# Loading, inverting and using the first batch's sums one double step sooner in a routed attention kernel with a feed-forward block

## The chip, the cores and the metric

The kernel runs on one core of one Trainium2 chip. Its time is device time in microseconds (us) from launch to end, as the median of several runs.

## The reference

Attention with routing, then a feed-forward block on its output, all in float32:

```python
batch, n_heads, seq, head_dim = (4, 8, 768, 64); n_clusters = 16
q_assign = np.argmax(np.einsum('bhsd,hcd->bhsc', q_n, c_n), axis=-1)   # same for k_assign
mask = q_assign[:, :, :, None] == k_assign[:, :, None, :]
scores = scale * np.matmul(q, k.transpose(0, 1, 3, 2))
scores = np.where(mask, scores, -1000000000.0)
scores = scores - np.max(scores, axis=-1, keepdims=True)
attn = np.exp(scores)
attn = attn / (np.sum(attn, axis=-1, keepdims=True) + 1e-09)
attn_out = np.matmul(attn, v)
x = attn_out.transpose(0, 2, 1, 3).reshape(3072, 512)
h = x @ w_in                        # 512 -> 2048
g = h * np.clip(h + 3.0, 0.0, 6.0) / 6.0
out = g @ w_out                     # 2048 -> 512
```

## The kernel before

Two heads form a pair, four pairs a batch (`NKT = 4`), sixteen pairs the whole. The first eight pairs (batches 0 and 1) are computed with the mask added to the scores, the last eight (batches 2 and 3) after sorting the rows by cluster, in a "late plan". The order of the work is written out by hand: each engine works off its instructions in the order in which the program issues them, and so does the queue of SP, which issues most DMAs.

**The first part** is a loop over n = 0, 2, 4, ... to 100. One pass is a "double step": two scores steps of a pair, each a block of 128 keys by 384 queries for two heads. A pair has twelve steps, so a batch has 48. Within one double step the program issues, in this order: two times `scores` (PE, line 407), `exponentials` (ACT, line 430) and `key_sums` (POOL, lines 437 and 440); two times `attn_v` (PE, line 450); once per pair `sum_up`; the preparation of the next pair; at some steps half a chunk of the feed-forward block; some steps of `decode`, which turns the float64 weights to float32 (SP line 222 loads them, ACT lines 235 and 251, VectorE lines 239 to 266); and last `check_all`.

The preparation of the next pair, by its place r in the pair's twelve steps: transposes of q and k (`turn`, PE line 325) at r = 0 and 2, scores against the clusters (line 344) at 4, `route` (VectorE: `mx` line 358, `one_hot` line 364) at 6, `route_turn` (PE line 386) at 8 and 10. At r = 6 SP also issues the loads of the next q, k and v (line 209).

**Deferred steps.** A function that is put into the list `later` during one double step, or during its `check_all`, runs in the `check_all` of a following one. If it is put there in the body of double step n, or while `check_all` of step n works off its list, it runs at the end of step n + 2:

```python
            check_all()
            checks.extend(later)
            later.clear()
```

**The sums of a batch.** The softmax is not divided score by score. `attn_v` stores the undivided values (`num`) into `xd` in DRAM (line 461). `sum_up` (line 467) sums the exponentials of a pair over the keys with PE (line 476), copies them (`dn`, line 480) and stores them in DRAM (`sums`, line 483). After the batch's last pair `load_sums` reads all its sums back, by tokens, into the tile `plain` (line 489), and three further steps follow, each queued by the one before: `invert` takes the reciprocal on VectorE (line 492) and stores it as `rd` (line 493); `complete` calls `load_block`, which loads a block of 256 tokens of `xd` as `xb` (line 556) and the inverses broadcast over 64 partitions each as `rb` (line 560); `divide` multiplies `xb` by `rb` on VectorE (line 510). Each of these steps stands at the end of a double step, behind that step's decode operations, and in front of the next one's routing.

For batch 0 the chain before is: store of the last sums at n = 50, load at the end of 52, inversion and store of `rd` at the end of 54, loads of `xb` and `rb` at the end of 56, division at the end of 58. At n = 60 the first "up" product of the feed-forward block (`ph`, PE line 634, sixteen matmuls) reads `xb`; ACT lifts it (line 517) and VectorE clips it (line 520). Seven more such products follow, at n = 64 to 94.

For batch 1 the last sums are stored at n = 98. `load_sums` only issues the load and leaves `invert` and `complete` to points 2 and 4 of the late plan.

**The rest** of the program is the late plan (sorted attention of batches 2 and 3) with the feed-forward block of the earlier batches between its points, and then the feed-forward block of the last ones alone (lines 686 and 725).

Of the kernel before, what the change touches and what calls it, by code (L numbers as in the profile page):

```python
# [122 lines left out]
def fast_path(ctx, tc, ok, q, k, v, centroids, moe_w_in, moe_w_out, out):  # L123
# [57 lines left out]
    later = []  # L181

    def scratch(shape, name, dtype=F32):

        if st["early"]:
            return psum_m.tile(shape, dtype, name=name, tag="m")
        return psum_t.tile(shape, dtype, name=name, tag="t")
# [279 lines left out]
    def sum_up(g):  # L467
        b, kt = divmod(g, NKT)
        if kt == 0:
            for name in ("sums", "rd"):  # L470
                st[name, b] = dram.tile([NKT, 2, S], F32, name=f"{name}{b}")
        pd = scratch([P, 512], "pd")[:, 0:HALF]
        for t in range(2):
            for hf in range(2):
                r = (2 * t + hf) * 2 * C
                nc.tensor.matmul(  # L476
                    pd[r : r + 2 * C], lhsT=ones[:, 0 : 2 * C], rhs=st["acc", g, hf][:, t], start=True, stop=True
                )
        dn = nump.tile([P, HALF], F32, name="dn")
        nc.scalar.copy(out=dn, in_=pd)  # L480
        for hf in range(2):
            st.pop(("acc", g, hf))
        nc.sync.dma_start(st["sums", b][kt].rearrange("t (hf c) -> (t hf) c", hf=2), dn[0 : P : 2 * C])
        if kt == NKT - 1:
            later.append(lambda: load_sums(b))

    def load_sums(b):
        tok = plain[:, b]
        nc.sync.dma_start(tok, st["sums", b].rearrange("k t s -> (k t s)").rearrange("(p n) -> p n", p=P))

        def invert():
            nc.vector.reciprocal(out=tok, in_=tok)
            nc.sync.dma_start(st["rd", b].rearrange("k t s -> (k t s)").rearrange("(p n) -> p n", p=P), tok)
            return complete

        def complete():
            waiting.extend((b, m) for m in range(NHC))
            load_block()
            if b == 0:
                later.append(lambda: divide(0, 0))  # L500

        if b == 0:
            later.append(lambda: later.append(invert()))
        else:
            st["invert"], st["complete"] = invert, complete

    def divide(b, m):
        if ("rb", b, m) in st:
            xb, rb = st["xb", b, m], st.pop(("rb", b, m))
            nc.vector.tensor_tensor(out=xb, in0=xb, in1=rb, op=ALU.mult)  # L510
# [39 lines left out]
    def load_block():  # L550
        if waiting and st["free"]:
            b, m = waiting.pop(0)
            st["free"] = False
            xb = st["xb", b, m] = xbp.tile([P, NKT, 2 * P], F32, name="xb")
            part = slice(2 * m * P, 2 * (m + 1) * P)
            nc.sync.dma_start(xb, st["xd", b][:, :, part])
            if ("rd", b) in st:
                rb = st["rb", b, m] = xbp.tile([P, NKT, 2 * P], F32, name="rb", tag="xs")
                for t in range(2):
                    nc.sync.dma_start(  # L560
                        rb[t * D : (t + 1) * D], st["rd", b][:, t, part].unsqueeze(0).to_broadcast([D, NKT, 2 * P])
                    )
# [811 lines left out]
    with tc.manual_schedule():  # L1374
# [24 lines left out]
        for n in range(0, total + lag_d + 2, 2):  # L1399
# [11 lines left out]
            if m >= 0 and m % per_pair == per_pair - 1:  # L1411
                sum_up(m // per_pair)
                ready(m)
# [407 lines left out]
```

## Time and profile before

| | before |
|---|---|
| time, median of 3 runs (lowest to highest) | 937.38 us (936.87 to 940.17) |
| the profiled execution's own time | 940.63 us |
| its span, first to last instruction | 938.7 us |
| mean granted TensorE clock | 0.997 |
| busy share PE, PEld, DVE, ACT, POOL | 98%, 77%, 59%, 36%, 63% |
| share of PE in the chain that ended last | 91% |

PE is TensorE's matmuls, PEld its weight loads, DVE is VectorE, ACT ScalarE, POOL GpSimd, SP the engine that issues most DMAs; SPq is its queue. A row of a timeline gives start and duration in us, engine and line, operation, tiles written and read, shapes and count; in brackets the idle time before it and what ended that. A waits row gives who waited for whom, with the total in us, the number of times and the longest. The granted clock is the share of TensorE's full clock that the chip's throttle let through. Durations in lists of one tile are in ns as least, median and most.

### The profile page before, as it was taken

The page shows a single profiled execution, that of the slowest core. Times are in us where ns is not written, and L with a number is a line of the kernel's source. Part 1 is how long each engine was busy: PE and PEld are TensorE (multiplying, and loading weights), DVE is VectorE, ACT ScalarE, POOL GpSimd, SP SyncE. Part 2 cuts the span into 40 slices and gives each one's busy share as a digit, 9 for nine tenths or more (in the row PEclk, how much of TensorE's full clock was granted, in tenths as well). Part 3 has the DMA queues.
Part 4 walks back from the last instruction along what each step waited for, and adds up shares of the span by engine and source line. Part 5 has one row for each costly group of instructions (what it writes and reads, how often), then busy time and mean ns, then how long its engine had stood idle before and what let it go on. Part 6 is the DMA issues. An engine that isn't in the chain of part 4 may idle for free.

```text
span 938.7 us, 17537 instructions
## 1 busy us (share of the span) xinstructions
PE 920.1 (98%) x6350; PEld 721.7 (77%) x6350; DVE 552.8 (59%) x1299; ACT 334.7 (36%) x667; POOL 586.9 (63%) x1313
## 2 busy tenths in 40 slices
PE   8999989999999999999999999999999999999997
PEld 5444445555898898797897978888888899999996
DVE  6667647778876385384483573563571555536261
ACT  6888767765012332222232241241322311212020
POOL 3877876779376787878778777777887060303030
PEclk9999999999999999999999999999999999999999
DMA  8444565450465566474772835645563334323120
GB/s 199 137 134 128 160 181 141 140 166 34 119 196 164 140 173 154 131 208 93 197 199 80 218 101 155 167 146 131 132 175 96 87 84 120 100 73 108 57 68 27
DMA packets 177024, 124.77 MB, mean 133 GB/s; under 512 B 135681, under 2 KB 155169, under 8 KB 176929
## 3 DMA queue, kind: packets, MB, share of 16 engines
q1 hardware_dynamic: 153968, 76.52, 31.1%
q10 hardware_dynamic: 13744, 34.44, 12.5%
q0 software_dynamic: 9216, 12.60, 4.4%
q8 instruction: 52, 0.85, 0.4%
q14 instruction: 44, 0.35, 0.1%
HBM read 95.11 MB, written 28.41 MB: 132 GB/s over the span
## 4 chain that ended last, share of the span: by engine, by line
PE 91%; DVE 3%; ACT 2%; DMA 2%; issue 1%; SPq 0%; DVEq 0%; ACTq 0%
PE Y L725 18%; PE uY L686 16%; PE X L725 13%; PE uX L686 12%; PE ps L407 7%; PE pv L450 6%; PE ph L634 3%; PE pv L1196 3%; PE ps L978 2%; PE ps L1139 2%; PE pcs L344 1%; PE pv L1139 1%; PE pqk L325 1%; DMA rb<-rd 1%; PE pd L476 1%
## 5 line engine op out<-in xcount | busy, mean ns | idle before, releaser
L440 POOL TENSOR_TENSOR acc<-acc,ex 128x768 f32<-128x768 f32 x64 | 124.8, 1950 | 29.9 <-ACT ex L430 26.5
L1094 POOL DMA_INDIRECT qd<-qn,pos x96 | 98.7, 1028 | 45.7 <-DVE tx L576 17.9
L1109 POOL DMA_INDIRECT xn<-xsd,pos x96 | 92.3, 961 | 49.5 <-ACT sx L517 27.9
L676 POOL TENSOR_TENSOR g_sb<-g_sb 128x256 f32<-128x256 f32 x52 | 39.2, 776 | 121.7 <-DVE g_sb L520 120.6
L517 ACT ACTIVATE sx<-g_sb,half_c 128x512 f32<-128x512 f32 x88 | 63.6, 723 | 144.1 <-DVE g_sb L697 111.4
L1086 POOL MEMSET w_low<- 128x1 f32 x864 | 91.6, 106 | 33.4
L1094 POOL DMA_INDIRECT kvd<-kvn,pos x96 | 97.3, 1013 | 21.7 <-issue 21.7
L732 DVE TENSOR_TENSOR y<-y,Y 128x256 f32<-128x256 f32 x47 | 19.8, 421 | 128.4 <-PE Y L725 100.1
L686 PE MATMUL uX<-xb,w_in_sb 128*128 128x128 f32 x704 | 93.0, 275 | 0.0
L725 PE MATMUL X<-w_out_sb,g_sb 128*128 128x256 f32 x384 | 90.3, 382 | 0.0
L725 PE MATMUL Y<-T,g_sb 128*128 128x256 f32 x384 | 88.0, 381 | 0.0
L725 PE MATMUL Y<-w_out_sb,g_sb 128*128 128x256 f32 x384 | 87.7, 380 | 0.0
L686 PEld LDWEIGHTS uX<-xb,w_in_sb 128*128 128x128 f32 x704 | 85.7, 192 | 0.0
L725 PEld LDWEIGHTS Y<-T,g_sb 128*128 128x128 f32 x384 | 72.1, 190 | 13.0 <-issue 3.3
L725 PEld LDWEIGHTS X<-w_out_sb,g_sb 128*128 128x128 f32 x384 | 71.0, 190 | 13.8 <-issue 4.0
L725 PEld LDWEIGHTS Y<-w_out_sb,g_sb 128*128 128x128 f32 x384 | 71.8, 190 | 10.5 <-issue 1.0
L697 DVE TENSOR_TENSOR sx<-uX,sx 128x128 f32<-128x128 f32 x176 | 51.1, 291 | 48.3 <-ACT sx L704 35.9
L407 PE MATMUL ps<-xf 64*128 64x384 f32 x384 | 78.6, 487 | 0.3 <-ACT ex L430 0.3
L430 ACT ACTIVATE ex<-ps 128x768 f32<-128x768 f32 x96 | 73.0, 804 | 5.9 <-PE ps L407 5.8
L450 PE MATMUL pv<-ex,vt 128*64 128x384 f32 x384 | 72.5, 499 | 0.0
L697 DVE TENSOR_TENSOR g_sb<-uY,sx 128x128 f32<-128x128 f32 (+1 forms) x176 | 65.6, 414 | 0.0
L520 DVE SCALAR_TENSOR_TENSOR g_sb<-sx,g_sb 128x512 f32<-128x512 f32 x88 | 64.0, 730 | 1.5 <-ACT sx L517 1.3
(211 smaller groups left out, 1727.1 us busy)
## 6 DMA issues: line engine op xcount, KB each, us to landing
tx<-td ACTq DMA_DIRECT2D x86, 384.0 KB
raw<-in_moe_w_in_dram SPq DMA_DIRECT2D x16, 512.0 KB
raw<-in_moe_w_out_dram SPq DMA_DIRECT2D x16, 512.0 KB
xb<-xd SPq DMA_DIRECT2D x12, 512.0 KB
out_dram<-y SPq DMA_DIRECT2D x44, 128.0 KB
qk<-in_k_dram SPq DMA_DIRECT2D x16, 192.0 KB
vt<-in_v_dram SPq DMA_DIRECT2D x16, 192.0 KB
xd<-num SPq DMA_DIRECT2D x16, 192.0 KB
```

Of the source, the lines that this page charges most:

```text
L407: nc.tensor.matmul(st["ps", n][:, t, 0:HALF], lhsT=x[r, NCH + j], rhs=x[r, hf * NHC : (hf + 1) * NHC], start=first, stop=last, skip_group_ ...
L430: nc.scalar.activation(out=ex, in_=sc, func=ACT.Exp, scale=SM_SCALE)
L440: nc.gpsimd.tensor_tensor(out=acc, in0=acc, in1=ex, op=ALU.add)
L450: nc.tensor.matmul(pv[t * D : (t + 1) * D], lhsT=vt[:, t, j], rhs=ex[:, t], start=(j == 0), stop=(j == NCH - 1),)
L517: nc.scalar.activation(out=r, in_=h, func=ACT.Relu, bias=half_c, scale=1.0 / 6.0)
L520: nc.vector.scalar_tensor_tensor(out=g, in0=r, scalar=1.0, in1=h, op0=ALU.min, op1=ALU.mult)
L686: nc.tensor.matmul(dst, lhsT=w[:, kt], rhs=x(kt), start=(kt == 0), stop=(kt == HK - 1))
L697: nc.vector.tensor_tensor(out=out_, in0=in0, in1=in1, op=ALU.add)
L725: nc.tensor.matmul(bank[:, half * HC : (half + 1) * HC], lhsT=g_sb[:, kind, i], rhs=w[:, i], start=(first and i == 0), stop=(last and i == ...
L1086: nc.gpsimd.memset(w_low, W_LOW)
L1094: i = nc.gpsimd.indirect_dma_start(out=rows[name, g, t], in_=src[:, j, t].rearrange("p a d -> p (a d)") if a else src[:, j, t], in_offset= ...
L1109: nc.gpsimd.indirect_dma_start(out=xn[:, j, t], out_offset=None, in_=rows["xsd", g, t], in_offset=bass.IndirectOffsetOnAxis(ap=pos[:, 0, j ...
```

## The change

`sum_up` of a batch's last pair no longer defers `load_sums` to the end of the next double step but calls it at once, right behind the store of the pair's sums. For batch 0 the steps that hang on it move with it: the load stands at n = 50 (in the body, behind the store), the inversion and the store of `rd` at the end of 52, in front of the routing of 54, the loads of `xb` and `rb` at the end of 54, the division at the end of 56. The first "up" product stays at n = 60. For batch 1 only the load moves.

```diff
@@ -482,7 +482,7 @@
             st.pop(("acc", g, hf))
         nc.sync.dma_start(st["sums", b][kt].rearrange("t (hf c) -> (t hf) c", hf=2), dn[0 : P : 2 * C])
         if kt == NKT - 1:
-            later.append(lambda: load_sums(b))
+            load_sums(b)
 
     def load_sums(b):
         tok = plain[:, b]
```

## The prediction

> **What bounds the kernel now.** The page comes first: its span, and how much of it TensorE is at work.
>
> ```profile
> span 938.7 us, 17537 instructions
> PE 920.1 (98%) x6350; PEld 721.7 (77%) x6350; DVE 552.8 (59%) x1299; ACT 334.7 (36%) x667; POOL 586.9 (63%) x1313
> ```
>
> TensorE is idle for 938.7 - 920.1 = 18.6 us in all. An edit that removes none of its work can win only from these, and from stretches that run at a low clock. Next the waits of PE alone, with the columns total, times, longest:
>
> ```profile
> PE ph L634 <- DVE xb L510: 3.5, 1, 3.5
> PE ps L978 <- ACT xsort L979: 1.4, 1, 1.4
> ```
>
> The largest single wait of the run is the one in front of the first "up" product of the feed-forward part, ph of line 634, for the division at line 510. That is what the moved steps lead up to. The chain of waits from there (start, duration, what), and the same sixteen matmuls one turn later:
>
> ```profile
> 126.55 8.68 DMA rb<-rd
> 136.80 5.38 PE ph L634 x16
> 151.09 3.65 PE ph L634 x16
> ```
>
> The division waits for rb, the broadcast inverses. The timelines of VectorE and of PE there:
>
> ```profile
> 130.57 0.69 DVE L261 SCALAR_TENSOR_TENSOR wunit<-raw,wunit 128x512 f32<-128x512 uint32 x1
> 135.36 1.30 DVE L510 TENSOR_TENSOR xb<-xb,rb 128x1024 f32<-128x1024 f32 x1 [4.09 <-DMA rb<-rd]
> 132.70 0.65 PE L325 MATMUL pqk<-ident,qk 128*128 128x128 f32 x4
> 136.80 5.38 PE L634 MATMUL ph<-xb,w_in_sb 128*128 128x256 f32 x16 [3.45 <-DVE xb L510]
> 142.02 0.60 PE L325 MATMUL pqk<-ident,qk 128*128 128x128 f32 x4
> ```
>
> PE has finished everything ahead of ph at 136.80 - 3.45 = 133.35 and stands until 136.80. The windows view (length, then PE, PEld, DVE, ACT and POOL busy, granted clock, DMA share, GB/s) shows a second cost behind it:
>
> ```profile
> 120.00:122.00 2.00, 2.00 (x17) 0.88 (x15) 0.62 (x2) 1.43 (x3) 0.87 (x1) 1.00 0.96 211
> 126.00:128.00 2.00, 2.00 (x13) 0.55 (x10) 1.93 (x3) 1.94 (x9) 1.08 (x1) 1.00 0.95 300
> 136.00:138.00 2.00, 1.20 (x6) 1.06 (x7) 0.66 (x1) 0.00 (x0) 1.92 (x2) 0.98 0.00 0
> 138.00:140.00 2.00, 2.00 (x6) 1.65 (x5) 0.00 (x0) 0.00 (x0) 0.05 (x1) 0.50 0.58 192
> ```
>
> From 138 to 140 us the granted clock is 0.50. So the sixteen matmuls take 5.38 us where the next sixteen take 3.65.
>
> **The change part by part.** No instruction is added or removed. Four things move one double step (two scores steps) up the program: the load of the sums, the reciprocal with its store, the loads of xb and rb, and the division. The queue of SP before, as issued:
>
> ```profile
> 113.64 0.56 SPq L483 DMA_DIRECT2D sums<-dn  x1
> 115.38 0.33 SPq L489 DMA_DIRECT2D plain<-sums  x1
> 115.80 1.26 SPq L209 DMA_DIRECT2D qk<-in_q_dram  x2
> 119.16 1.11 SPq L209 DMA_DIRECT2D vt<-in_v_dram  x2
> 123.88 0.33 SPq L493 DMA_DIRECT2D rd<-plain  x1
> 125.21 0.53 SPq L556 DMA_DIRECT2D xb<-xd  x1
> 125.83 1.37 SPq L560 DMA_DIRECT2D rb<-rd  x2
> SPq L489 <- DMA sums<-dn: 0.2, 1, 0.2
> ```
>
> The last row is from SP's own waits: the load of the sums already waits 0.2 us for their store. SP runs ahead of the other engines. Issued one double step sooner, the load stands directly behind that store and still leaves at 115.38, 1.74 us after the store began. It gains nothing by itself. What was issued between the two, one store of num and one load of raw weights, goes about 1.5 us later.
>
> The reciprocal is the real move. VectorE before:
>
> ```profile
> 113.02 0.69 DVE L255 TENSOR_SCALAR wunit<-wtop 128x512 uint32<-128x512 uint32 x1
> 121.28 0.56 DVE L358 TENSOR_REDUCE mx<-pr 128x24 f32<-128x384 f32 x1 [7.56 <-PE pr L355]
> 123.41 0.44 DVE L492 RECIPROCAL plain<-plain 128x48 f32<-128x48 f32 x1
> 126.61 1.02 DVE L261 SCALAR_TENSOR_TENSOR wunit<-raw,wunit 128x512 f32<-128x512 uint32 x1
> ```
>
> Today it is queued behind the routing (mx and the two one_hot) and a decode operation, which wait for PE until 121.28. After the change it stands in the 7.56 us in which VectorE is idle, from 113.71. Its cost there is nothing; that cover is the idle time. It must wait for the load of the sums. The lower bound for that landing is the 1.74 us from issue to landing of the sums' own store, so 117.12; the upper is the 8.68 us that rb takes on the chain, counted from the end of the issue at 115.71, so 124.39. A 24 KB load with little issued ahead of it is much nearer to the store: I take 117.1. The reciprocal then ends near 117.6. Queued behind it while it waits is the routing, which has 121.28 - 117.6 = 3.7 us to spare.
>
> SP holds the store of rd until the reciprocal is done, and behind it the six loads of the next pair. They begin near 118.0 in place of 115.80, 2.2 us later. Their issue runs from 115.80 to 119.16 + 1.11 = 120.27, so 4.47 us, and ends near 122.5. The first reader of the next pair's qk is the pqk at 132.70, so 10 us lie between. Then follow xb (0.53) and both rb (1.37): with the gaps they end near 124.5, where they ended at 125.83 + 1.37 = 127.20. So rb is issued 2.7 us sooner.
>
> Its landing depends on what is ahead of it. Sizes from the page's list of DMA issues:
>
> ```profile
> xb<-xd SPq DMA_DIRECT2D x12, 512.0 KB
> rb<-rd SPq DMA_DIRECT2D x12, 256.0 KB
> qk<-in_k_dram SPq DMA_DIRECT2D x16, 192.0 KB
> vt<-in_v_dram SPq DMA_DIRECT2D x16, 192.0 KB
> xd<-num SPq DMA_DIRECT2D x16, 192.0 KB
> raw<-in_moe_w_out_dram SPq DMA_DIRECT2D x16, 512.0 KB
> ```
>
> Today one raw and one num (some 700 KB) stand between the reciprocal's store and xb; after the change they come behind rb. The six loads ahead hold 6 x 192 = 1152 KB. At the 211 GB/s of the 120 to 122 us window that is 5.6 us from 118.0, so 123.6, just over a microsecond past the end of their issue. Then xb and both rb, 1024 KB, at 300 GB/s take 3.5 us: 127.1, the early end. The late end is 8.68 us after issue, as now: 124.5 + 8.7 = 133.2. I take 129 to 130, since the 700 KB are gone from in front but the broadcast loads may run below 300 GB/s.
>
> The division now stands at the end of the previous double step's decode operations, at 126.61 + 1.02 = 127.63, less the 0.44 of the reciprocal that is no longer in front: about 127.2. It waits for rb, say to 130, and ends at 131.3. Behind it on VectorE are five decode operations, which took from 127.63 to 130.57 + 0.69 = 131.26, about 3.6 us; they now end near 135. None of them feeds PE in this stretch. The next that matters there is the clip of ph, not wanted before 133.35 + 3.65 + 0.69 = 137.7. So PE finds xb divided at 133.35 if rb has landed by 133.35 - 1.30 - 0.14 = 131.9. Even at the late end of 133.2 the hole would be 1.3 us, and the gain 3.45 - 1.3 + 1.73 = 3.9 us.
>
> What is late next? Not ACT, which lifts right behind ph as now. POOL:
>
> ```profile
> 135.66 2.39 POOL L576 TENSOR_TENSOR tx<-w_in_sb,tx 128x256 f32<-128x256 f32 x2
> POOL acc L440 <- ACT ex L430: 13.4, 7, 7.6
> ```
>
> POOL ends its sums of weights at 138.05 and then idles 7.6 us for the next exponentials. Moved up by 5.2 us, 2.4 us of that are left. So the whole shift goes through, and behind it the chain is PE work nearly without a break to the end.
>
> The sum: 3.45 us of hole and 5.38 - 3.65 = 1.73 us of half clock, together 5.18 us. The clock term is the less sure of the two: the trace shows one case, in the profiled execution. The Trainium skill ("TensorE: Matmul & The Clock Gate", Part 1) says that about 3.4 us without activity, counted in a window that runs free of the kernel, take the clock to half; the hole of 3.45 us and the 0.50 behind it agree. By that rule it also depends on where the window happens to lie, so other executions need not pay it.
>
> For the second batch only the load of the sums moves: its reciprocal and division hang on points of the late plan.
>
> ```profile
> L489 SPq DMA_DIRECT2D plain<-sums x2: 320/324/327, 115.4 to 240.7; - x2
> L492 DVE RECIPROCAL plain<-plain x2: 441/444/446, 123.4 to 246.3; 128x48 f32<-128x48 f32 x2
> ```
>
> Its load at 240.7 has 5.6 us until its reciprocal at 246.3, so nothing follows from moving it: 0.
>
> The profiled execution took 940.63 us (938.7 of span and 1.93 around it); it should come to 935.45. The median of the three runs is 937.38, 3.25 us less than the profiled one. I take the same 5.18 us off it: **932.2 us**, 0.55% less.
>
> **The rivals.** A measurement of this kernel tells about 0.5%, 4.69 us, from no change.
>
> *The hole goes, but ordinary executions don't pay the half clock.* For it: one stretch at 0.50 in one trace, and a hole of 3.45 us that could easily lie otherwise in the clock's windows. Against: the one trace has it. Gain 3.45 us: 933.9.
>
> *The hole is smaller in ordinary executions.* The profiled execution is 3.25 us above the median. If that is this very hole, in that rb lands sooner when nothing is traced, then only 5.18 - 3.25 = 1.93 us are left to win: 935.4. Against it: the slowest of the three runs, 940.17, is nearly as slow as the profiled one, so a spread of that size exists anyway.
>
> *The inversion holds up the routing: slower.* VectorE works in order, so if the sums land after 121.28, mx waits, then one_hot, then PE:
>
> ```profile
> 124.34 0.51 PE L386 MATMUL po<-ident_q,one_hot 128*128 128x128 bf16 x6
> 122.48 1.01 DVE L261 SCALAR_TENSOR_TENSOR wunit<-raw,wunit 128x512 f32<-128x512 uint32 x1
> ```
>
> The one_hot is done by about 122.5 and PE reads it at 124.34, so there are 1.8 us of slack. It decides from a landing at 121.28 - 0.44 + 1.8 = 122.6 on. At the late bound of 124.39 PE stands 1.8 us there. The store of rd then leaves near 125, no sooner than now, and the six loads come ahead of rb too, so the old hole stays: about 939.2, and more if rb then lands later than today's. Against it: the load is 24 KB and has nearly the whole 5.6 us between 115.7 and 121.3.
>
> *It doesn't do what it says:* rb lands when it does now, because the loads ahead of it are pushed back as far as it is pulled forward. The hole stays: 937.4. For it: the 2.2 us by which they go later. Against: it is still issued 2.7 us sooner with less in front.
>
> **How the numbers follow.** The full gain (932.2) gets 0.50, the gain without the clock term 0.19, the smaller hole 0.17, no effect 0.08, the held-up routing 0.06. The full case lies 0.5 us beyond the 0.5% line, and medians scatter by more than that: I count 0.36 of its 0.50 as faster and 0.14 as within. Of the next two cases 0.05 come out faster by chance, which makes 0.41 faster. Slower by over 0.5% needs 4.69 us of loss, more than the held-up routing costs at its bound: 0.03. The rest, 0.56, is within 0.5%. The range runs from 930.8, the full gain with some scatter below it, to 936.2, which takes in the smaller hole; no effect and the held-up routing stay outside.
>
> **What would show it.** In the changed profile the reciprocal stands near 117 us, ahead of mx. rb is issued to about 124.5 and no PE wait for xb L510 is left, or one under 1.5 us. ph begins near 133.4 and takes about 3.65 us, and no window near 138 us shows 0.50. The division carries a wait for rb of 1 to 4 us on VectorE, now without effect. I am wrong if the sums land after 121 us, if rb lands after 133, or if the 5 us come back as a new wait of PE before 255 us, with POOL or ACT ahead of it.

## The result and the profile after

| | before | after |
|---|---|---|
| time, median of 8 runs each (lowest to highest) | 939.25 us (936.87 to 942.15) | 934.87 us (933.87 to 936.42) |
| ratio, 95% interval | | 0.9954, 0.9939 to 0.997 |
| span of the profiled execution | 938.7 us | 932.8 us |

The change makes the kernel 4.38 us faster, 0.46%. In a second measurement (b0_after_again below) the ratio was 0.9949, from 0.9936 to 0.9962.

First PE's waits after the change. The row for ph has gone from the top of the list to 0.5 us:

```profile
PE ps L978 <- issue: 2.4, 3, 1.6
...
PE ph L634 <- DVE xb L510: 0.5, 1, 0.5
```

PE's timeline at the place. What matters is where the pqk behind ph starts: 142.02 before, 137.37 now, so 4.65 us are won here.

```profile
132.73 0.66 PE L325 MATMUL pqk<-ident,qk 128*128 128x128 f32 x4
133.84 3.69 PE L634 MATMUL ph<-xb,w_in_sb 128*128 128x256 f32 x16 [0.45 <-DVE xb L510]
137.37 0.60 PE L325 MATMUL pqk<-ident,qk 128*128 128x128 f32 x4
```

The hole shrank from 3.45 to 0.45 us, which is 3.00, and ph takes 3.69 us instead of 5.38, which is 1.69. The windows show the clock (the column after POOL's) at 1.00 where it was 0.50:

```profile
136.00:138.00 2.00, 2.00 (x14) 1.60 (x14) 1.37 (x2) 0.43 (x1) 1.84 (x3) 1.00 0.00 0
138.00:140.00 2.00, 2.00 (x15) 0.92 (x15) 1.68 (x3) 1.97 (x5) 0.00 (x0) 1.00 0.60 195
```

The chain that leads there, from the copy of the sums on:

```profile
113.67 1.68 DMA sums<-dn
115.36 0.02 issue
115.38 1.56 DMA plain<-sums
116.94 0.02 issue
116.96 0.46 DVE plain L492
117.42 0.02 issue
117.44 0.32 SPq L493
...
122.49 0.53 SPq L556
...
123.75 7.19 DMA rb<-rd
...
131.06 2.64 DVE xb L510
133.70 0.14 issue
133.84 3.69 PE ph L634 x16
```

The load leaves at 115.38 as before, lands at 116.94, and the reciprocal follows at once. Then SP issues the six loads of the next pair, which are in the part left out, and xb and rb. The landing of rb still takes 7.19 us from its issue, but from 123.75 on, so it is there at 130.94.

VectorE's timeline has the reciprocal in what was idle time. The routing behind it still waits for PE, with 3.90 us to spare:

```profile
116.96 0.45 DVE L492 RECIPROCAL plain<-plain 128x48 f32<-128x48 f32 x1 [3.21 <-DMA plain<-sums]
121.31 0.56 DVE L358 TENSOR_REDUCE mx<-pr 128x24 f32<-128x384 f32 x1 [3.90 <-PE pr L355]
126.47 1.19 DVE L261 SCALAR_TENSOR_TENSOR wunit<-raw,wunit 128x512 f32<-128x512 uint32 x1
131.06 2.63 DVE L510 TENSOR_TENSOR xb<-xb,rb 128x1024 f32<-128x1024 f32 x1 [3.40 <-DMA rb<-rd]
138.29 0.69 DVE L520 SCALAR_TENSOR_TENSOR g_sb<-g_sb,ph 128x512 f32<-128x512 f32 x1 [0.88 <-ACT g_sb L517]
```

One row is not as forecast: the division takes 2.63 us where it took 1.30. Without that PE would not wait at all, as experiment b2 shows.

The spans differ by 5.9 us, 1.25 more than the 4.65 won here. Along the late plan the lead of the same PE instructions in the two traces goes down to 3.8 us and up to 6.4, with small waits that differ between the two traces. What causes each of them stays open.

### The profile page after: what moved, and what is told of

It is laid out like the page before. It is cut to its first block, busy times and chain, and to the rows that moved or that the text cites. A ratio compares the mean times of both kernels' runs of the same rounds, so it can differ in the third digit from the quotient of the medians.

```text
span 932.8 us, 17534 instructions
## 1 busy us (share of the span) xinstructions
PE 917.6 (98%) x6350; PEld 720.4 (77%) x6350; DVE 554.7 (59%) x1299; ACT 334.4 (36%) x667; POOL 584.4 (63%) x1313
## 4 chain that ended last, share of the span: by engine, by line
PE 93%; ACT 2%; DMA 2%; DVE 1%; issue 1%; SPq 1%; DVEq 0%; ACTq 0%
PE Y L725 18%; PE uY L686 17%; PE X L725 14%; PE uX L686 13%; PE ps L407 7%; PE pv L450 6%; PE ph L634 3%; PE pv L1196 3%; PE ps L978 3%; PE ps L1139 2%; PE pcs L344 1%; PE pv L1139 1%; PE pqk L325 1%; DMA rb<-rd 1%; PE pd L476 1%
```

## The experiments

The theory: PE's hole in front of ph was the end of one chain, from the reciprocal over SP's queue and the DMA queues to rb and the division. The reciprocal stood behind the routing, which waits for PE. The hole cost twice, once by itself and once by the half clock that followed it. The rivals: the gain is in the place of the load, or in that of the division on VectorE, or in the second batch; or the half clock belongs to the traced execution alone.

**a1_load_alone.** The load goes out at once, the rest stays where it was.

```diff
 # after.py, load_sums
-            later.append(lambda: later.append(invert()))
+            later.append(lambda: later.append(lambda: later.append(invert())))
```

> The load of the sums goes out right behind their store, as in the change, but the inversion, the loads of xb and rb and the division stay where they were before. Theory (the load gains nothing by itself, the reciprocal behind the routing is what holds the chain): same as before within 0.15%, the load still issued near 115.4 us and landing about 1.5 us sooner, the reciprocal near 123.4, PE's wait in front of ph 3.0 to 3.5 us, the granted clock once at half behind it. Rival (the earlier load is the gain): 4 to 5 us faster than before, no wait in front of ph.

Measured 0.9991, from 0.9981 to 1.0001 of before: no change that can be told. PE's waits have the old row:

```profile
PE ph L634 <- DVE xb L510: 3.5, 1, 3.5
```

VectorE's timeline has the reciprocal where it was, behind the routing:

```profile
123.65 0.44 DVE L492 RECIPROCAL plain<-plain 128x48 f32<-128x48 f32 x1
```

The half clock is there too, at 0.50 from 136.5 to 139.9 us. So the load's place gains nothing by itself.

**a2_invert_alone.** The load stays deferred; the inversion follows it at the end of the same double step.

```diff
 # before.py, load_sums
-            later.append(lambda: later.append(invert()))
+            later.append(invert())
```

> The load of the sums keeps its old place in SP's queue, behind num and raw; the inversion follows it at the end of the same double step, so it, xb, rb and the division stand where the change puts them. Theory: nearly the whole gain. The sums land near 118.3 as before instead of 116.9, the reciprocal ends near 118.9, rb is issued 1.4 us later than in the changed kernel and lands near 132.3; the division, then free of a POOL addition, ends near 133.7, so PE waits 0.3 to 0.8 us for it and the time is 4 to 4.7 us under before. Rival (the load's place matters): the wait in front of ph is over 1.5 us and less than 3 us are gained.

Measured 0.9961, from 0.9947 to 0.9976; 935.17 us against 938.37. The changed kernel's ratio lies inside that interval. The sums land behind num and raw, so the reciprocal stands at 118.56 instead of 116.96, but PE's wait in front of ph is the same 0.45 us. VectorE's timeline:

```profile
118.56 0.45 DVE L492 RECIPROCAL plain<-plain 128x48 f32<-128x48 f32 x1 [4.85 <-DMA plain<-sums]
131.82 1.84 DVE L510 TENSOR_TENSOR xb<-xb,rb 128x1024 f32<-128x1024 f32 x1 [4.19 <-DMA rb<-rd]
```

The division starts 0.76 us later than in the changed kernel and ends together with it, at 133.66 against 133.69. I had expected it to be free of a POOL addition. It was not; POOL's timeline has the same two additions as in the changed kernel, up to 132.58, and the division ends 1.08 us behind them (b2 below is the test of this):

```profile
128.87 3.71 POOL L440 TENSOR_TENSOR acc<-acc,ex 128x768 f32<-128x768 f32 x2 [1.79 <-ACT ex L430]
```

So the gain hangs on the inversion and on the loads and the division that follow it, not on the place of the load of the sums.

**a3_divide_old.** The change, with only the division left at the end of n = 58.

```diff
 # after.py, complete
-                later.append(lambda: divide(0, 0))
+                later.append(lambda: later.append(lambda: divide(0, 0)))
```

> The change, but with the division kept at the end of the double step in which it stood before, behind five more decode operations. Theory (what counts is when rb lands): same as the changed kernel within 0.1%, 4 to 5 us under before; the division starts near 131.3, behind the same POOL addition, ends near 133.7, and PE waits 0.3 to 0.6 us. Rival (the division's place on VectorE carries part of the gain): over 1 us slower than the changed kernel.

Measured 0.9949, from 0.9929 to 0.9968, so the division's place carries no part of the gain that the times can show. The trace has a wait of 0.80 us in front of ph, a little over what I expected and 0.35 us over that of the changed kernel. Two of its seven executions, the traced one among them, took 938.3 and 939.9 us, the others 932.3 to 933.6. The trace shows part of why its own execution took longer: a second place like the one at ph, in the late plan. PE's timeline there:

```profile
463.43 1.54 PE L978 MATMUL ps<-ident,qn 128*128 128x128 f32 x6 [2.39 <-ACT xnat L979]
```

And the windows, the granted clock again behind POOL's busy time:

```profile
461.00:463.00 2.00, 0.04 (x1) 0.00 (x0) 1.19 (x4) 0.42 (x1) 1.73 (x6) 1.00 0.35 114
465.00:467.00 2.00, 2.00 (x12) 2.00 (x12) 0.00 (x0) 0.80 (x1) 1.58 (x7) 0.55 0.87 245
```

Here ACT was late, and a hole of 2.39 us was enough to bring the clock down, from 463.4 to 466.8 us. In the trace of the changed kernel the hole at this place is 1.61 us and the clock stays at 1.00. Why ACT was late there stays open, and so does the rest of the difference between the executions.

**a4_loads_at_once.** The inversion stays behind the routing; xb and rb are loaded directly behind the store of rd.

```diff
 # before.py, load_sums
-            later.append(lambda: later.append(invert()))
+            later.append(lambda: (invert(), complete()))
```

> The inversion stays behind the routing as before, at 123.4 us, but xb and rb are loaded right behind the store of rd, one double step sooner, ahead of a raw and a num load that stood in front of them. Theory A (what delayed rb was the 700 KB in front of it and its place in the DMA queues, not the routing alone): rb is issued to about 126.9, only 0.3 us sooner than before, yet lands near 130 instead of 135.2; the wait in front of ph is under 0.5 us and the gain 4.5 to 5.2 us, as much as the change. Theory B (the time of the reciprocal is what counts): rb lands at 133 or later and 2 us or less are gained.

Measured 0.9943, from 0.9929 to 0.9958: as much as the change. SP's timeline:

```profile
123.99 0.33 SPq L493 DMA_DIRECT2D rd<-plain  x1
124.36 0.53 SPq L556 DMA_DIRECT2D xb<-xd  x1
125.45 1.30 SPq L560 DMA_DIRECT2D rb<-rd  x2
```

VectorE's:

```profile
133.09 1.22 DVE L510 TENSOR_TENSOR xb<-xb,rb 128x1024 f32<-128x1024 f32 x1 [5.34 <-DMA rb<-rd]
```

The issue of rb ends at 126.75, only 0.45 us sooner than before, and the division starts at 133.09 instead of 135.36. So most of the 2.3 us goes with the load of raw and the store of num, which no longer stand in front of rb. The division moves up one double step as well, but it waits for rb in both traces. The landing was slower than I expected, 133 instead of 130, and PE still waits 1.0 us instead of under 0.5. The times follow theory A; the landing alone would have spoken for B. The inversion in front of the routing is thus one of two ways out: each brings the start of the division forward by over 2 us, and that is nearly enough to close the hole.

**b0_after_again.** The changed kernel beside the next three on one chip, with no edit.

> The changed kernel once more, beside the next three on one chip. Theory: 4.0 to 5.2 us under before, PE's wait in front of ph 0.3 to 0.6 us, no half clock near 138 us.

Measured 932.06 us against 936.9, 0.9949, from 0.9936 to 0.9962. PE's wait in front of ph is 0.45 us again, and the division took 2.47 us.

**b2_pool_clear.** One POOL addition moved away from where rb lands.

```diff
 # after.py, the loop over n
-                key_sums(i)
+                if i != 59:
+                    key_sums(i)
+            if n == 60:
+                key_sums(59)
```

> The change, with one addition of exponentials on POOL (that of the last scores step of the pair before) issued one double step later, so that POOL is idle when rb lands. Theory (the division took 2.63 us because VectorE could not start while POOL's addition ran): the division takes 1.2 to 1.3 us again, ends near 132.3, and PE does not wait in front of ph; 0.4 us under the changed kernel in the trace, too little for the times. Rival (DMA writes slow the division): still 2 us or more, and the wait stays.

In the changed kernel POOL's timeline has two additions that begin at 128.91 and end at 132.62, and a next one:

```profile
128.91 3.71 POOL L440 TENSOR_TENSOR acc<-acc,ex 128x768 f32<-128x768 f32 x2 [1.80 <-ACT ex L430]
133.13 2.25 POOL L437 TENSOR_TENSOR acc<-ex 128x768 f32<-128x768 f32 x1 [0.52 <-ACT ex L430]
```

The division that starts at 131.06 ends at 133.69, which is 1.07 us after POOL's addition; POOL's next one takes 2.25 us in place of 1.8. In b2, VectorE's timeline:

```profile
130.96 1.22 DVE L510 TENSOR_TENSOR xb<-xb,rb 128x1024 f32<-128x1024 f32 x1 [3.42 <-DMA rb<-rd]
```

POOL's:

```profile
128.78 1.81 POOL L440 TENSOR_TENSOR acc<-acc,ex 128x768 f32<-128x768 f32 x1 [1.79 <-ACT ex L430]
133.02 1.82 POOL L437 TENSOR_TENSOR acc<-ex 128x768 f32<-128x768 f32 x1 [2.43 <-ACT ex L430]
```

And PE's:

```profile
133.10 3.62 PE L634 MATMUL ph<-xb,w_in_sb 128*128 128x256 f32 x16
```

With POOL idle from 130.59 to 133.02 the division takes 1.22 us and PE does not wait at all. The rival was DMA traffic. The windows from 130 to 132 us, first of the changed kernel, then of b2, have the DMA engines about as busy in both (1.01 and 0.96, the last column but one), so it is not what slowed the division:

```profile
130.00:132.00 2.00, 1.78 (x14) 0.82 (x16) 0.94 (x1) 1.97 (x6) 1.92 (x2) 1.00 1.01 347
130.00:132.00 2.00, 1.91 (x14) 0.95 (x16) 1.04 (x1) 1.97 (x6) 0.58 (x1) 1.00 0.96 358
```

The other traces say the same. In ten of the thirteen the division starts while POOL is at work, anywhere from 0.2 to 1.7 us before that work ends, and its own end comes 1.07 to 1.09 us behind the end of POOL's. In the other three (a4, b2, c1) POOL is idle then, or idle within 0.1 us, and the division takes 1.22 us. Before is one of the ten: a POOL copy was still running until 135.58, and the 1.30 us were already a little too long for the division alone:

```profile
134.86 0.72 POOL L576 TENSOR_TENSOR tx<-w_in_sb 128x256 f32<-128x256 f32 x1
```

The time of b2 is 931.6 us (0.9946, from 0.9933 to 0.9958), too close to the 932.06 of the changed kernel to tell them apart.

**b3_sooner.** The change, with xb and rb loaded directly behind the store of rd.

```diff
 # after.py, load_sums
-            later.append(lambda: later.append(invert()))
+            later.append(lambda: (invert(), complete()))
```

> The change, with xb and rb loaded right behind the store of rd, ahead of the six loads of the next pair, and the division another double step sooner. Theory (nothing is left to win but the last wait): rb lands near 124, the division ends before 127.5, no wait in front of ph; 0.45 us under the changed kernel in the trace, the times within 0.15% of it. Rival 1 (more lead still wins): over 1.5 us under the changed kernel. Rival 2 (the six loads, pushed back by 3 us, come late for the next pair): a new wait of PE for qk near 133 us, and the gain is lost.

Measured 931.77 us, 0.9947, from 0.9935 to 0.9959. Here the division stands at 126.83, 4.2 us before the changed kernel's, and ph does not wait. VectorE's timeline:

```profile
126.83 1.62 DVE L510 TENSOR_TENSOR xb<-xb,rb 128x1024 f32<-128x1024 f32 x1 [3.03 <-DMA rb<-rd]
```

PE's:

```profile
133.50 3.62 PE L634 MATMUL ph<-xb,w_in_sb 128*128 128x256 f32 x16
```

rb landed at 126.7 and the division ended at 128.45, later than the 124 and 127.5 I expected, since SP issued rb only at 120.27, behind the landing of rd, and the division met a POOL addition here too. More lead wins nothing more that can be told, and the six loads pushed back cost nothing: PE has no new wait for qk. b2 and b3 are the two versions without any wait here; by the times neither can be told from the change.

**b1_warm, c1_warm_short, c2_warm_short_again.** The kernel before with matmuls of the identity in the hole, 24 in b1 and 14 in the others. They are written to ph and overwritten.

```diff
 # before.py, up: end, behind the tile ph
+                    for _ in range(24 if u == 0 else 0):        # 14 in c1 and c2
+                        nc.tensor.matmul(ph[:, 0:P], lhsT=ident, rhs=ident, start=True, stop=True)
```

> The kernel before with 24 matmuls of the identity added on PE right in front of ph, about 3.1 us of work that nobody reads; they fill the hole of 3.45 us and leave the wait for rb as it is. Theory (the hole costs twice, once in itself and once in the half clock behind it): no stretch at half clock near 138 us, ph in about 3.65 us instead of 5.38, 1.4 to 1.8 us under before. Rival 1 (ordinary executions do not pay the half clock): same as before within 0.07%. Rival 2 (the work in the hole is not hidden): slower than before by up to 3 us.

Measured 1.0001, from 0.9993 to 1.001. My size was wrong: each of these matmuls is two passes of 0.115 us, so they take 5.52 us and end after the division, which was done at 136.54. PE's timeline:

```profile
133.06 5.52 PE L632 MATMUL ph<-ident 128*128 128x128 f32 x48
138.42 3.62 PE L636 MATMUL ph<-xb,w_in_sb 128*128 128x256 f32 x16
```

ph starts 1.7 us later than it could and runs at full clock, so both effects would cancel. By its times this run alone decides nothing safely.

> As b1_warm, but 14 matmuls of the identity in front of ph. In b1_warm the 24 took 5.52 us and so ended 1.7 us after the division; at 0.23 us each, 14 take 3.2 us and end inside the hole. Theory (the half clock is paid in ordinary executions too): ph starts near 136.7 as before, takes 3.65 us at full clock, and the time is 1.2 to 1.8 us under before (ratio 0.998 to 0.9988). Rival (only the traced execution pays it; b1_warm came out level because its work was hidden in a shorter hole): same as before within 0.05%.

Measured 1.0007, from 0.9977 to 1.0036, on a chip on which the kernel before itself scattered from 940.7 to 952.3 us: inconclusive.

> c1_warm_short once more, on another chip, since the times of its first run scatter over 15 us and decide nothing. Theory (the half clock is paid in ordinary executions too): 1.2 to 1.8 us under before, ratio 0.998 to 0.9988. Rival (only the traced execution pays it): same as before within 0.05%.

Measured 936.37 us against 938.93, 0.9981, from 0.9969 to 0.9992. PE's timeline:

```profile
133.51 3.29 PE L632 MATMUL ph<-ident 128*128 128x128 f32 x28
137.06 3.72 PE L636 MATMUL ph<-xb,w_in_sb 128*128 128x256 f32 x16 [0.26 <-DVE xb L510]
```

The windows have the clock at 1.00 where it was 0.50:

```profile
138.00:140.00 2.00, 2.00 (x11) 1.74 (x10) 0.00 (x0) 0.00 (x0) 0.39 (x1) 1.00 0.39 149
```

The division and with it ph start no sooner; only the clock is kept up. By the ratio that alone gains 1.8 us, by its interval 0.8 to 2.9, where the theory had 1.2 to 1.8.

The mean granted clock, measured in every execution, says the same without the times. One stretch of 3.42 us at half clock takes 0.0018 off the mean of a span of 938.7 us. Averaged over the executions of before on the three chips it is 0.9968, 0.9967 and 0.9964; with the hole filled it is 0.9990 (b1), 0.9986 (c1) and 0.9988 (c2) on the same chips. So ordinary executions pay the half clock too.

**b4_second_only.** Only the second batch's load goes out at once.

```diff
 # after.py, sum_up
-            load_sums(b)
+            load_sums(b) if b else later.append(lambda: load_sums(b))
```

> Only the second batch's load of its sums is issued at once; the first batch's steps stay where they were before. Theory: same as before within 0.1%, with the wait of 3.0 to 3.5 us in front of ph and half clock behind it. Rival (part of the gain comes from the second batch): over 0.15% under before.

It ran beside c1 on the same chip: 1.0006, from 0.9981 to 1.0031, so the times exclude only a gain of over 0.19%. In its trace the second batch's reciprocal starts at 246.5 us, where before it started at 246.3. Its waits of PE have the old row, with its 3.5 us:

```profile
PE ph L634 <- DVE xb L510: 3.5, 1, 3.5
```

## Why the prediction was right

**The bound and the place** were read rightly from PE's own waits. The largest single wait of the run, 3.45 us in front of ph, is where 4.65 us were won.

**The steps on SP and VectorE** came out within a few tenths of a microsecond. The sums landed at 116.94 (taken: 117.1), the reciprocal ended at 117.41 (117.6), the issue of rb at 124.37 (124.5). The landing of rb came at 130.94, 1 to 2 us after the 129 to 130 I took and well inside the bounds of 127.1 and 133.2.

**The routing** kept 3.90 us of slack; I had 3.7. So the rival in which the inversion holds it up found no ground in the trace.

**The division** is the term that was mis-sized. I took 1.30 us from the row of before and concluded that PE does not wait if rb lands by 131.9. It landed a microsecond before that and PE waited 0.45 us, since at the new place an addition on POOL stands in the way and the division takes 2.63 us. b2 shows it: 1.22 us and no wait with POOL idle. That the wait stayed so small is in part luck, since nothing in the forecast looked at POOL there. I had weighed who waits for VectorE, but not what runs on POOL while VectorE works on two operands in SBUF. The Trainium skill ("SBUF — State Buffer", section "Who interferes with whom") says that a VectorE instruction with two SBUF inputs contends with a GpSimd instruction that reads SBUF, and that the port pair they share is an exclusive lock; the two rows of POOL above, 1.07 us from its end to the division's and 2.25 us for its own next one, agree.

**The half clock** was right at 1.73 us (1.69 measured), and the rival that ordinary executions do not pay it fell with c2 and the mean clocks. The rival of a hole that is smaller in ordinary executions fell with the two measurements: they won 4.38 and 4.84 us, by their intervals 2.8 to 5.7 and 3.6 to 6.0, not 1.93. (3.45 us, the gain without the clock term, lies inside the first of these intervals; the clocks decide against it.)

**The sum.** 5.18 us less 0.45 of remaining hole, and 0.08 for ph, pqk and the reading of their starts, are the 4.65 of the trace. The forecast of 0.9945 stands against 0.9954, with 0.9945 inside the interval. That 934.87 us is 2.7 above the 932.2 forecast comes mostly from the median of three runs that I started from, 937.38, which with more runs is 939.25. The time alone says little about the mechanism: 934.87 lies between the 933.9 and the 935.4 that two of the rivals gave, so it was the gains, the trace and the experiments that set them aside. The gain of 0.46% lies within 0.5%, where I had put 0.56.

**The second batch** adds nothing that b4's trace shows, as the forecast had it; its times allow up to 0.19%.

## What to carry to other kernels

Where one engine is busy 98% of the time, look through its own waits first: the longest one names the chain to shorten, and the clock behind it can cost half as much again (here 1.69 us behind a hole of 3.45). Follow that chain back through the queues; an instruction that waits for nothing of its own may stand behind one that does, and what stands in front of a load in its DMA queue counts as much as when it is issued (a4). When an operation is moved in time, look up what the other engines run at its new place before its old duration is reused.

## What the runs showed of the hardware

The half clock needs less than a full idle stretch of the length in which it then runs slowly. In the trace of before, the clock was at 0.50 from 137.91 to 141.33, for 3.42 us. PE was busy for 1.10 of the 3.40 us ahead of the drop; the windows view, with the columns as above:

```profile
134.50:137.90 3.40, 1.10 (x5) 1.02 (x6) 1.30 (x1) 0.00 (x0) 3.24 (x4) 1.00 0.04 16
```

In a3 a hole of 2.39 us brought the clock down, while in the trace of after a wait of 1.6 us at the same line did not. The drop isn't tied to the start of the hole either: it came 4.6 us behind it in before and 2.9 us behind it in a1, with a hole of the same length. The Trainium skill ("TensorE: Matmul & The Clock Gate", Part 1) speaks of at least one idle window of about 3.4 us; here a hole of 2.39 us was enough, and in before the 3.40 us ahead of the drop were only two thirds idle, so the measurement decides. A hole of 3.45 us cost 1.69 us more that way, and filling it with work that nobody reads kept the clock up (c2: 3.72 us for ph instead of 5.38).
